# Batch 1 of a linear attention: v loaded ahead of a weight block, its kv three slots earlier, its h in whole blocks

## The chip, the cores and the metric

The kernel runs on one core of a Trainium2 chip. The core has five engines that run side by side: TensorE (PE: matrix products), VectorE (DVE), ScalarE (ACT: activation functions and copies), GpSimd (POOL) and SyncE (SP), which issues the loads here. The metric is the time of one execution on the device, in microseconds.

## What is computed

Eight batches, eight heads, 576 rows of 64. First a linear attention, then two dense layers with a gelu between them:

```python
def phi(x):
    return np.where(x > 0, x, np.exp(x) - 1.0) + 1.0
q_p, k_p = (phi(q), phi(k))
kv = np.einsum('bhsd,bhse->bhde', k_p, v)
z = np.sum(k_p, axis=2)
num = np.einsum('bhsd,bhde->bhse', q_p, kv)
den = np.einsum('bhsd,bhd->bhs', q_p, z)[..., None] + 1e-06
x = num / den            # then heads side by side: 4608 rows of 512
h = x @ w_in             # 512 x 2048
out = gelu_tanh(h) @ w_out   # 2048 x 512
```

## The kernel before

phi(x) is computed as min(exp(x), max(x + 1, 1)): an exp on ScalarE (`exp_of`, L207), an addition with a maximum on VectorE (`linear_of`, L218) and a minimum on VectorE (`least_of`, L232). v is cast to bf16 into `vp`, which has a column of ones behind every 64 values, so that kv also yields z. `kv_paired` (L257) makes the kv products of a batch, `kv_evac` (L287) copies them to the block-diagonal `kvbd`.

A batch's first 512 rows are four chunks of 128. For each chunk `nab` (L317, called `n` in the plan) multiplies the transposed q by `kvbd` into the pair of banks `ps_a`, and VectorE divides by the last column: a reciprocal and a product, which give x (L307, L309). `ps_a` exists once. `transpose_x` (L338, called `t`) transposes x on TensorE into a bank and ScalarE copies it to `xt`. The remaining 64 rows of each batch are gathered in `xt_rest`.

Then comes the dense part, `iteration(j)` (L661), for batch j: 16 blocks "h" (four matmuls of 128x512 each, and a gelu on ScalarE) and 16 steps "o" (four matmuls each: a tile t of 128 rows against a quarter u of w_out). In iteration 0 the o steps run quarter by quarter, u outside and t inside, so w_out's block u is first needed at slot 16 + 4u; in iteration 1 eight h come first, then eight o. There are 32 such slots in an iteration. The steps of the next batch's attention are hung behind slots by `at(j, slot, fn)` (L441) and run there in the order of their registration (`run`, L445). Each engine executes its instructions in the order in which this program emits them; the order of the engines among each other follows from semaphores.

Batch 0 is worked off by `first_batch` (L377) at the start, with some products on zeros to keep TensorE busy (`keep_warm`). There h's first three blocks are begun chunk by chunk as `h_quarter` (L363), four matmuls of width 128 for each chunk of xt. Batch 1 is planned by `plan_second` (L449) into iteration 0: `maps` behind slot 15 (exps, additions, minima, and a part of the casts of w_out), `transpose_q` behind slot 23, the casts of v behind 25, kv behind 26, n and t from slot 27 on, with quarters of two h blocks between them in slots 30 and 31.

All loads are issued by SP in the order of the code (L147 to L172), into the pool `pld` of seven buffers, which are handed round: a load waits until the eighth tile before it has been read. Weights come as fp32 in eight blocks of 1024 KB and are cast to bf16 by `cast_w_in` and `cast_w_out` (L136, L142), most of them on GpSimd. w_out's third block is index 2 in the code (quarter u = 2), its fourth is index 3.

Of the kernel before, what the change touches and what calls it, by code (L numbers as in the profile page):

```python
# [9 lines left out]
BF16 = mybir.dt.bfloat16  # L10
# [5 lines left out]
def kernel(  # L16
# [21 lines left out]
    C = 4  # L38
# [50 lines left out]
    def load_pairs(name, src, b, us=slice(0, NP)):  # L89
        s = src[b].rearrange("h s d -> (h s d)").rearrange("(u n f) -> n u f", n=P, f=J * D)  # L90
        nc.sync.dma_start(out=ld[name, b][:, us, :], in_=s[:, us, :])  # L91

    def load_q_paired(b, parities=(0, 1)):
        src = q[b, :, 0:MAIN, :].rearrange("(u a) (p c) d -> p a u (c d)", a=2, c=C)
        for a in parities:
            nc.sync.dma_start(out=ld["q", b][:, NP * a : NP * (a + 1), :], in_=src[:, a])  # L96
# [33 lines left out]
    def load_w(wr, i):  # L130
        t = pld.tile([P, 4, 512], FP32, name="w_st", tag="ld")
        w_st[wr is w_in_r, i] = t
        src = wr[:, :, 512 * i : 512 * (i + 1)] if wr is w_in_r else wr[:, 4 * i : 4 * i + 4, :]
        nc.sync.dma_start(out=t, in_=src)
# [15 lines left out]
    for n in "qkv":  # L150
        ld_tile(n, 0)
    for s in range(2):
        load_pairs("k", k, 0, halves[s])
        load_q_paired(0, (s,))
    for s in range(2):
        load_pairs("v", v, 0, halves[s])
    for i in range(4):
# [4 lines left out]
    load_w(w_out_r, 1)  # L162
    ld_tile("k", 1)
    load_pairs("k", k, 1)
    load_w(w_out_r, 2)
    ld_tile("v", 1)
    load_pairs("v", v, 1)
    load_w(w_out_r, 3)
    load_batch(2)
    load_main("q", q, 3)  # L170
    load_main("k", k, 3)
# [186 lines left out]
    def gelu(g, m, h_ps):  # L358
        nc.scalar.activation(g[:, m, :], h_ps, AF.Gelu_apprx_tanh)  # L359

    h_begun = {0: {}, 1: {}}

    def h_quarter(j, c, blocks):  # L363
        for m in range(blocks):
            if c == 0:
                h_begun[j][m] = bank("h_ps", [P, MAIN])
            h_mm(h_begun[j][m], xts[j], m, slice(P * c, P * (c + 1)))

    def xt_chunk(j, c):
        return xts[j][:, :, P * c : P * (c + 1)]  # L370
# [6 lines left out]
    def first_batch():  # L377
        w_ps = bank("w_ps", [P, 512])

        def keep_warm(n):  # L380
            for _ in range(n):
                nc.tensor.matmul(w_ps, lhsT=warm[:, 0:P], rhs=warm)  # L382

        qt = pt.tile([P, C, NP, P], BF16, name="qt")
        qs = (slice(0, 4), slice(4, 8))

        def transpose_q(s, fn):
            t_ps = bank("t_ps", [P, C, 2, P], BF16)
            for i in range(2):
                for c in range(C):  # L390
                    h = 4 * s + 2 * i
                    nc.tensor.transpose(
                        t_ps[:, c, i, :], phi["q", 0][:, c, h : h + 2, :], ident
                    )
            fn(out=qt[:, :, 2 * s : 2 * s + 2, :], in_=t_ps)

        keep_warm(18)
        for s in range(2):
            for n, hs in (("k", halves[s]), ("q", qs[s])):
                exp_of(n, 0, hs)  # L400
                linear_of(n, 0, hs)
                least_of(n, 0, hs)
        transpose_q(0, nc.scalar.copy)
        keep_warm(10)
        transpose_q(1, nc.scalar.copy)
        keep_warm(2)
        for ii in range(2):
            cast_v_paired(0, halves[ii], nc.vector.tensor_copy)
        for ii in range(2):
            kv_ps = [bank("kv_ps", [P, E]) for _ in range(2)]  # L410
            kv_paired(0, ii, lambda a, ii: kv_ps[a])
            for a, fn in enumerate((nc.vector.tensor_copy, nc.scalar.copy)):
                block = slice(2 * a + ii, 2 * a + ii + 1)
                kv_evac(0, block, kv_ps[a].rearrange("p (i e) -> p i e", i=1), fn)
        gelu_table()
        for s in range(2):
            cast_w_in(0, nc.gpsimd.tensor_copy, slice(256 * s, 256 * s + 256))
        for i in range(1, 4):
            cast_w_in(i, nc.gpsimd.tensor_copy)
        for i in range(2):  # L420
            cast_w_out(i, nc.gpsimd.tensor_copy)
        cast_w_out(2, nc.gpsimd.tensor_copy, slice(0, 2))
        keep_warm(2)

        xts[0] = pt.tile([P, NP, MAIN], BF16, name="xt")
        x = {0: nab(qt[:, 0], 0), 1: nab_in_banks(qt[:, 1], 0)}
        for c in range(C):
            transpose_x(x[c], xt_chunk(0, c), nc.scalar.copy)
            if c + 2 < C:
                x[c + 2] = (nab, nab_in_banks)[c % 2](qt[:, c + 2], 0)  # L430
            if c > 0:
                h_quarter(0, c - 1, 3)
        h_quarter(0, C - 1, 3)

    first_batch()

# [12 lines left out]
    def plan_second():  # L449
        b = 1  # L450
        x = {}

        def maps():
            for n in "qk":
                exp_of(n, b)
            gelu_table()
            for n in "qk":
                linear_of(n, b)
            least_of("q", b)
            cast_w_out(2, nc.vector.tensor_copy, slice(2, 4))  # L460
            least_of("k", b)

        def transpose_q():
            qts[b] = pt.tile([P, C, NP, P], BF16, name="qt")
            for s in range(2):
                t_ps = bank("t_ps", [P, 2, NP, P], BF16)
                for c in range(2):
                    for i in range(NP):
                        nc.tensor.transpose(  # L469
                            t_ps[:, c, i, :],  # L470
                            phi["q", b][:, 2 * s + c, 2 * i : 2 * i + 2, :],
                            ident,
                        )
                nc.scalar.copy(qts[b][:, 2 * s : 2 * s + 2], t_ps)

        def casts():
            cast_v_paired(b, halves[0], nc.vector.tensor_copy)
            cast_v_paired(b, halves[1], nc.scalar.copy)

        def kv():  # L480
            kv_ps = [bank("kv_ps", [P, 2, E]) for _ in range(2)]
            for ii in range(2):
                kv_paired(b, ii, lambda a, ii: kv_ps[a][:, ii, :])
            for a, fn in enumerate((nc.vector.tensor_copy, nc.scalar.copy)):
                kv_evac(b, slice(2 * a, 2 * a + 2), kv_ps[a], fn)

        def last_w_out():
            cast_w_out(3, nc.scalar.copy, slice(0, 1))
            cast_w_out(3, nc.vector.tensor_copy, slice(1, 2))
            cast_w_out(3, nc.gpsimd.tensor_copy, slice(2, 4))  # L490

        def n(c):
            x[c] = nab(qts[b][:, c], b)

        def t(c):
            if c == 0:
                xts[b] = pt.tile([P, NP, MAIN], BF16, name="xt")
            transpose_x(x[c], xt_chunk(b, c), nc.scalar.copy)

        at(0, 15, maps)  # L500
        at(0, 23, transpose_q)
        at(0, 25, casts)
        at(0, 26, kv)
        at(0, 26, last_w_out)
        at(0, 27, n, 0)
        at(0, 28, n, 1)
        at(0, 28, t, 0)
        at(0, 29, n, 2)
        at(0, 29, t, 1)
        at(0, 30, h_quarter, b, 0, 2)  # L510
        at(0, 30, n, 3)
        at(0, 30, t, 2)
        at(0, 31, h_quarter, b, 1, 2)
        at(0, 31, t, 3)
        at(0, 31, h_quarter, b, 2, 2)
        at(0, 31, h_quarter, b, 3, 2)

    def plan_prepare(b, s_linear, s_exp):
        rest = b % 2 == 0
# [141 lines left out]
    def iteration(j):  # L661
        xt = xts[j] if j < B else xt_rest
        g = pg.tile([P, MM, MAIN], BF16, name="g")
        hs = [("h", m) for m in range(MM)]
        if j == 0:
            steps = hs + [("o", t, u) for u in range(4) for t in range(C)]
        elif j == 1:
            os = [[("o", t, u) for u in us for t in range(C)] for us in ((0, 1), (2, 3))]
            steps = hs[:8] + os[0] + hs[8:] + os[1]
        else:  # L670
            steps = hs + [("o", t, u) for t in range(C) for u in range(4)]
        o_pss = {}
        for slot, step in enumerate(steps):
            if step[0] == "h":
                m = step[1]
                h_ps = h_begun.get(j, {}).get(m)
                if h_ps is None:
                    h_ps = bank("h_ps", [P, MAIN])
                    h_mm(h_ps, xt, m)
                gelu(g, m, h_ps)  # L680
            else:
                t, u = step[1:]
                if j == B and t == C - 1:
                    if u == 0:
                        last_tile(g, t)
                    continue
                if u == 0:
                    o_pss[t] = bank("o_ps", [P, d_model])
                o_mm(o_pss[t], g, t, u)
                if u == 3:  # L690
                    finish(j, t, o_pss[t])
            run(j, slot)
# [55 lines left out]
```

## Time and profile before

| what | us |
|---|---|
| median of 3 runs (289.17 to 289.42) | 289.2 |
| the profiled execution | 288.86 |
| its span | 286.9 |
| TensorE busy | 278.5 |
| ScalarE busy | 164.7 |
| VectorE busy | 107.8 |
| GpSimd busy | 18.4 |

The profile is of one execution. Busy times are sums over the span; a time such as "at 42.1" is counted from the span's start. In TensorE's timeline the durations of neighbouring matmuls overlap, since they are pipelined; the distance of two starts tells what the first one occupied. Loads keep the DMA engines full for the first 46 us (some 400 GB/s), and less after that. Iteration 0 runs from about 19 to 50 us, iteration 1 to about 80.

### The profile page before, as it was taken

How to read it: one execution, taken by the hardware profiler on the slowest of the kernel's cores; microseconds unless marked ns; L12 is line 12 of the kernel's file. 1: busy time of each engine (PE TensorE's matmuls, PEld its weight loads, DVE VectorE, ACT ScalarE, POOL GpSimd, SP SyncE). 2: the span in 40 equal slices, each digit the busy share in tenths (PEclk: the TensorE clock that was granted, in tenths of full speed). 3: DMA queues.
4: the chain of work that ended last, by engine and by line, in shares of the span. 5: the costliest groups of instructions: out<-in, count | busy, mean ns of one | idle time of the engine just before them, and what ended most of it. 6: DMA issues, size and time to landing. Idle time of an engine off the chain costs nothing.

```text
span 286.9 us, 4569 instructions
## 1 busy us (share of the span) xinstructions
PE 278.5 (97%) x1868; PEld 137.0 (48%) x1868; DVE 107.8 (38%) x180; ACT 164.7 (57%) x226; POOL 18.4 (6%) x25
## 2 busy tenths in 40 slices
PE   8789999999999999999999999999999999999994
PEld 2464456545445445544554455444544444444443
DVE  3850366633865282544247515640412010000001
ACT  4767886695966844684367735772572275027400
POOL 6066230000000000000000000000000000000000
PEclk9999999999999999999999999999999999999999
DMA  7999999956988969955799489735141210120022
GB/s 252 403 407 397 410 400 269 347 215 172 178 234 295 239 159 141 379 153 146 211 294 210 74 250 356 95 91 165 35 41 39 88 58 0 54 91 3 0 73 73
DMA packets 71379, 53.76 MB, mean 187 GB/s; under 512 B 42048, under 2 KB 62784, under 8 KB 71360
## 3 DMA queue, kind: packets, MB, share of 16 engines
q1 hardware_dynamic: 68656, 44.58, 55.4%
q10 hardware_dynamic: 2704, 8.91, 8.5%
q8 instruction: 14, 0.23, 0.3%
q14 instruction: 5, 0.04, 0.0%
HBM read 36.70 MB, written 9.44 MB: 161 GB/s over the span
## 4 chain that ended last, share of the span: by engine, by line
PE 93%; DMA 3%; DVE 1%; SPq 1%; ACT 1%; issue 0%; ACTq 0%
PE h_ps L349 44%; PE o_ps L642 43%; DMA v_x<-in_v_dram 3%; PE n_ps L294 3%; PE kv_ps L278 1%; PE t_ps L341 1%; SPq L91 1%; PE kv_ps L263 0%; SPq L96 0%; PE t_ps L469 0%; DVE x L330 0%; DVE vp L241 0%; DVE x L309 0%; ACT w_out_sb L143 0%; ACT xt L342 0%
## 5 line engine op out<-in xcount | busy, mean ns | idle before, releaser
L642 PE MATMUL o_ps<-w_out_sb,g 128*128 128x512 bf16 (+1 forms) x592 | 127.1, 373 | 0.2 <-ACT w_out_sb L143 0.2
L349 PE MATMUL h_ps<-xt,w_in_sb 128*128 128x512 bf16 (+1 forms) x572 | 118.0, 357 | 0.2 <-ACT xt L342 0.2
L359 ACT ACTIVATE g<-h_ps 128x512 bf16<-128x512 f32 x144 | 84.9, 597 | 46.6 <-PE h_ps L349 45.5
L642 PEld LDWEIGHTS <-g 128*128 128x128 bf16 x592 | 57.6, 98 | 65.4 <-issue 0.3
L349 PEld LDWEIGHTS <-w_in_sb 128*128 128x128 bf16 x636 | 57.5, 98 | 59.5 <-issue 0.7
L608 ACT COPY o_sb<-o_ps 128x512 f32<-128x512 f32 (+1 forms) x19 | 10.9, 574 | 61.5 <-PE o_ps L642 54.4
L608 DVE COPY o_sb<-o_ps 128x512 f32<-128x512 f32 (+1 forms) x18 | 12.1, 674 | 69.0 <-PE o_ps L642 69.0
L307 DVE RECIPROCAL r<-n_ps 128x8 f32<-128x8 f32 x34 | 7.0, 207 | 48.7 <-PE n_ps L294 48.7
L309 DVE TENSOR_TENSOR x<-n_ps,r 128x512 bf16<-128x512 f32 x34 | 23.5, 692 | 1.2
L212 ACT ACTIVATE k_e<-k_x 128x2048 bf16<-128x2048 f32 (+2 forms) x9 | 15.8, 1755 | 3.7 <-DMA k_x<-in_k_dram 3.7
L236 DVE TENSOR_TENSOR q_p<-q_p,q_e 128x2048 bf16<-128x2048 bf16 (+1 forms) x9 | 10.0, 1106 | 16.8 <-ACT q_e L212 16.5
L212 ACT ACTIVATE q_e<-q_x 128x2048 bf16<-128x2048 f32 (+1 forms) x9 | 15.5, 1721 | 0.5 <-DMA q_x<-in_q_dram 0.4
L349 PE MATMUL h_ps<-xt_rest,w_in_sb 128*128 128x512 bf16 x64 | 14.0, 379 | 0.0
L223 DVE TENSOR_SCALAR q_p<-q_x 128x2048 bf16<-128x2048 f32 (+1 forms) x9 | 9.9, 1100 | 10.0 <-DMA q_x<-in_q_dram 10.0
L223 DVE TENSOR_SCALAR k_p<-k_x 128x2048 bf16<-128x2048 f32 (+2 forms) x9 | 10.2, 1137 | 8.9 <-DMA k_x<-in_k_dram 8.9
L294 PEld LDWEIGHTS <-qt 128*128 128x128 bf16 x128 | 9.7, 98 | 7.0 <-DVE x L309 0.8
L294 PE MATMUL n_ps<-kvbd,qt 128*128 128x130 bf16 x128 | 12.7, 221 | 0.0
L290 DVE CAST kvbd<-kv_ps 64x260 bf16<-64x260 f32 (+2 forms) x18 | 6.6, 366 | 11.2 <-PE kv_ps L278 8.2
L236 DVE TENSOR_TENSOR k_p<-k_p,k_e 128x2048 bf16<-128x2048 bf16 (+2 forms) x9 | 10.2, 1132 | 1.4 <-ACT k_e L212 1.4
L382 PE MATMUL w_ps<-warm 128*128 128x512 bf16 x32 | 9.4, 449 | 1.2 <-DVE warm L177 1.2
L373 ACT ACT_TABLE_LOAD x8 | 10.3, 1283 | 0.1
L212 ACT ACT_TABLE_LOAD x8 | 10.3, 1283 | 0.1
(49 smaller groups left out, 95.3 us busy)
## 6 DMA issues: line engine op xcount, KB each, us to landing
out_dram<-o_sb ACTq DMA_DIRECT2D x16, 512.0 KB, 3.3
q_x<-in_q_dram SPq DMA_DIRECT2D x6, 1024.0 KB, 6.8
k_x<-in_k_dram SPq DMA_DIRECT2D x6, 1024.0 KB, 11.1
v_x<-in_v_dram SPq DMA_DIRECT2D x6, 1024.0 KB, 7.3
w_st<-in_moe_w_in_dram SPq DMA_DIRECT2D x4, 1024.0 KB, 14.0
w_st<-in_moe_w_out_dram SPq DMA_DIRECT2D x4, 1024.0 KB, 13.2
q_x<-in_q_dram SPq DMA_DIRECT2D x4, 512.0 KB, 9.3
k_x<-in_k_dram SPq DMA_DIRECT2D x2, 576.0 KB, 5.0
```

Source lines behind the costliest of these rows:

```text
L212: nc.scalar.activation(by_chunk(exps[name, b], hs), x[:, hs].rearrange("p h (c d) -> p h c d", d=D), AF.Exp,)
L223: nc.vector.tensor_scalar(by_chunk(phi[name, b], hs), x[:, hs].rearrange("p h (c d) -> p h c d", d=D), 1.0, 1.0, op0=ALU.add, op1=ALU.max,)
L236: nc.vector.tensor_tensor(p, p, e, op=ALU.min)
L294: nc.tensor.matmul(ns[i // 2][rows, 2 * E * (i % 2) : 2 * E * (i % 2 + 1)], lhsT=qt_c[:, i, rows], rhs=kvbd[:, i, :], skip_group_check=True,)
L307: nc.vector.reciprocal(r, n_v[:, :, :, D])
L309: nc.vector.tensor_tensor(x_view(x, paired), n_v[:, :, :, 0:D], r[:, :, :, None].to_broadcast([P, 2, NP, D]), op=ALU.mult,)
L349: nc.tensor.matmul(h_ps[:, ts], lhsT=w_in_sb[:, c, P * m : P * (m + 1)], rhs=xt[:, c, ts], start=(c == 0), stop=(c == KM - 1), skip_group_ ...
L359: nc.scalar.activation(g[:, m, :], h_ps, AF.Gelu_apprx_tanh)
L373: nc.scalar.preload_act_table_set("gelu_apprx_tanh_and_others")
L382: nc.tensor.matmul(w_ps, lhsT=warm[:, 0:P], rhs=warm)
L608: (nc.scalar.copy if on_scalar else nc.vector.tensor_copy)(dst, src)
L642: nc.tensor.matmul(o_ps, lhsT=g[:, m, P * t : P * (t + 1)], rhs=w_out_sb[:, m, fs], start=(m == 0), stop=(m == MM - 1),)
```

## The change

It has these parts.

- At the start, the loads of batch 0 go q half, k half, q half, k half, where before k's half came first in each pair; the exps, additions and minima of batch 0 follow in the same order.
- Batch 1's v is loaded ahead of w_out's third block.
- The third block's first half is cast on GpSimd within `maps`, behind the cast of the second half of batch 1's v, which moves from ScalarE to GpSimd. The first half of that v is cast on VectorE between the minima of q and k. VectorE casts the third block's second half behind k's minimum.
- The transposes of batch 1's q go to the pair of banks `ps_a` in one tile; kv stands right behind them, at slot 23. The gelu table is loaded behind kv's evacuation.
- n goes to slots 24 to 27, t to slots 25 to 28; within a slot, t of one chunk stands ahead of n of the next.
- w_out's fourth block is cast in halves on GpSimd and ScalarE, without VectorE.
- Batch 1 has no quarters of h: its blocks are all computed with width 512. Batch 0 keeps its own.

```diff
--- before.py
+++ after.py
@@ -150,8 +150,8 @@
     for n in "qkv":
         ld_tile(n, 0)
     for s in range(2):
+        load_q_paired(0, (s,))
         load_pairs("k", k, 0, halves[s])
-        load_q_paired(0, (s,))
     for s in range(2):
         load_pairs("v", v, 0, halves[s])
     for i in range(4):
@@ -162,10 +162,10 @@
     load_w(w_out_r, 1)
     ld_tile("k", 1)
     load_pairs("k", k, 1)
-    load_w(w_out_r, 2)
     ld_tile("v", 1)
     load_pairs("v", v, 1)
-    load_w(w_out_r, 3)
+    for i in range(2, 4):
+        load_w(w_out_r, i)
     load_batch(2)
     load_main("q", q, 3)
     load_main("k", k, 3)
@@ -358,13 +358,13 @@
     def gelu(g, m, h_ps):
         nc.scalar.activation(g[:, m, :], h_ps, AF.Gelu_apprx_tanh)
 
-    h_begun = {0: {}, 1: {}}
-
-    def h_quarter(j, c, blocks):
+    h_begun = {}
+
+    def h_quarter(c, blocks):
         for m in range(blocks):
             if c == 0:
-                h_begun[j][m] = bank("h_ps", [P, MAIN])
-            h_mm(h_begun[j][m], xts[j], m, slice(P * c, P * (c + 1)))
+                h_begun[m] = bank("h_ps", [P, MAIN])
+            h_mm(h_begun[m], xts[0], m, slice(P * c, P * (c + 1)))
 
     def xt_chunk(j, c):
         return xts[j][:, :, P * c : P * (c + 1)]
@@ -396,7 +396,7 @@
 
         keep_warm(18)
         for s in range(2):
-            for n, hs in (("k", halves[s]), ("q", qs[s])):
+            for n, hs in (("q", qs[s]), ("k", halves[s])):
                 exp_of(n, 0, hs)
                 linear_of(n, 0, hs)
                 least_of(n, 0, hs)
@@ -419,7 +419,6 @@
             cast_w_in(i, nc.gpsimd.tensor_copy)
         for i in range(2):
             cast_w_out(i, nc.gpsimd.tensor_copy)
-        cast_w_out(2, nc.gpsimd.tensor_copy, slice(0, 2))
         keep_warm(2)
 
         xts[0] = pt.tile([P, NP, MAIN], BF16, name="xt")
@@ -429,8 +428,8 @@
             if c + 2 < C:
                 x[c + 2] = (nab, nab_in_banks)[c % 2](qt[:, c + 2], 0)
             if c > 0:
-                h_quarter(0, c - 1, 3)
-        h_quarter(0, C - 1, 3)
+                h_quarter(c - 1, 3)
+        h_quarter(C - 1, 3)
 
     first_batch()
 
@@ -453,29 +452,24 @@
         def maps():
             for n in "qk":
                 exp_of(n, b)
-            gelu_table()
-            for n in "qk":
                 linear_of(n, b)
             least_of("q", b)
+            cast_v_paired(b, halves[0], nc.vector.tensor_copy)
+            cast_v_paired(b, halves[1], nc.gpsimd.tensor_copy)
+            least_of("k", b)
+            cast_w_out(2, nc.gpsimd.tensor_copy, slice(0, 2))
             cast_w_out(2, nc.vector.tensor_copy, slice(2, 4))
-            least_of("k", b)
 
         def transpose_q():
             qts[b] = pt.tile([P, C, NP, P], BF16, name="qt")
-            for s in range(2):
-                t_ps = bank("t_ps", [P, 2, NP, P], BF16)
-                for c in range(2):
-                    for i in range(NP):
-                        nc.tensor.transpose(
-                            t_ps[:, c, i, :],
-                            phi["q", b][:, 2 * s + c, 2 * i : 2 * i + 2, :],
-                            ident,
-                        )
-                nc.scalar.copy(qts[b][:, 2 * s : 2 * s + 2], t_ps)
-
-        def casts():
-            cast_v_paired(b, halves[0], nc.vector.tensor_copy)
-            cast_v_paired(b, halves[1], nc.scalar.copy)
+            t_ps = ps_a.tile([P, C, NP, P], BF16, name="t_ps", tag="a")
+            for c in range(C):
+                for i in range(NP):
+                    nc.tensor.transpose(
+                        t_ps[:, c, i, :], phi["q", b][:, c, 2 * i : 2 * i + 2, :], ident
+                    )
+                if c % 2 == 1:
+                    nc.scalar.copy(qts[b][:, c - 1 : c + 1], t_ps[:, c - 1 : c + 1])
 
         def kv():
             kv_ps = [bank("kv_ps", [P, 2, E]) for _ in range(2)]
@@ -483,11 +477,11 @@
                 kv_paired(b, ii, lambda a, ii: kv_ps[a][:, ii, :])
             for a, fn in enumerate((nc.vector.tensor_copy, nc.scalar.copy)):
                 kv_evac(b, slice(2 * a, 2 * a + 2), kv_ps[a], fn)
+            gelu_table()
 
         def last_w_out():
-            cast_w_out(3, nc.scalar.copy, slice(0, 1))
-            cast_w_out(3, nc.vector.tensor_copy, slice(1, 2))
-            cast_w_out(3, nc.gpsimd.tensor_copy, slice(2, 4))
+            cast_w_out(3, nc.gpsimd.tensor_copy, slice(0, 2))
+            cast_w_out(3, nc.scalar.copy, slice(2, 4))
 
         def n(c):
             x[c] = nab(qts[b][:, c], b)
@@ -499,21 +493,11 @@
 
         at(0, 15, maps)
         at(0, 23, transpose_q)
-        at(0, 25, casts)
-        at(0, 26, kv)
+        at(0, 23, kv)
+        for c in range(C):
+            at(0, 24 + c, n, c)
+            at(0, 25 + c, t, c)
         at(0, 26, last_w_out)
-        at(0, 27, n, 0)
-        at(0, 28, n, 1)
-        at(0, 28, t, 0)
-        at(0, 29, n, 2)
-        at(0, 29, t, 1)
-        at(0, 30, h_quarter, b, 0, 2)
-        at(0, 30, n, 3)
-        at(0, 30, t, 2)
-        at(0, 31, h_quarter, b, 1, 2)
-        at(0, 31, t, 3)
-        at(0, 31, h_quarter, b, 2, 2)
-        at(0, 31, h_quarter, b, 3, 2)
 
     def plan_prepare(b, s_linear, s_exp):
         rest = b % 2 == 0
@@ -673,7 +657,7 @@
         for slot, step in enumerate(steps):
             if step[0] == "h":
                 m = step[1]
-                h_ps = h_begun.get(j, {}).get(m)
+                h_ps = h_begun.get(m) if j == 0 else None
                 if h_ps is None:
                     h_ps = bank("h_ps", [P, MAIN])
                     h_mm(h_ps, xt, m)
```

## The prediction

> **What bounds the kernel now.** I read the chain of work that ended last first, then TensorE's timeline, then the timelines of VectorE, GpSimd and the loads.
>
> The shares of the chain, from the page:
>
> ```profile
> PE 93%; DMA 3%; DVE 1%; SPq 1%; ACT 1%; issue 0%; ACTq 0%
> ```
>
> So TensorE is the path from the first kv product to the end. DMA's 3% is the start: the first kv waits for the second half of batch 0's v. An edit can move the time in three ways only: through the start, through what TensorE has to do, or through gaps between its instructions. I looked for gaps at the places of the diff, by the start times on TensorE's timeline (start, duration, instruction, count, idle before it). Durations there overlap, so I take differences of starts.
>
> ```profile
> 38.55 1.06 PE L469 MATMUL t_ps<-ident,q_p 128*128 128x128 bf16 x16
> 39.45 2.75 PE L642 MATMUL o_ps<-w_out_sb,g 128*128 128x512 bf16 x12
> 42.13 0.78 PE L263 MATMUL kv_ps<-vp,k_p 64*64 64x65 bf16 x72
> 42.84 1.04 PE L642 MATMUL o_ps<-w_out_sb,g 128*128 128x512 bf16 x4
> 43.71 0.40 PE L294 MATMUL n_ps<-kvbd,qt 128*128 128x130 bf16 x4
> 44.29 1.02 PE L642 MATMUL o_ps<-w_out_sb,g 128*128 128x512 bf16 x4 [0.18 <-ACT w_out_sb L143]
> 45.15 0.40 PE L294 MATMUL n_ps<-kvbd,qt 128*128 128x130 bf16 x4
> 45.39 0.38 PE L341 MATMUL t_ps<-ident,x 128*128 128x128 bf16 x4
> 45.61 1.03 PE L642 MATMUL o_ps<-w_out_sb,g 128*128 128x512 bf16 x4
> 46.58 0.41 PE L294 MATMUL n_ps<-kvbd,qt 128*128 128x130 bf16 x4
> ...
> 51.18 5.79 PE L349 MATMUL h_ps<-xt,w_in_sb 128*128 128x128 bf16 x32 [0.23 <-ACT xt L342]
> 56.80 7.07 PE L642 MATMUL o_ps<-w_out_sb,g 128*128 128x512 bf16 x32
> ```
>
> A block of o (four matmuls) takes 0.86 from start to start, four transposes 0.22, an n 0.24, kv 0.71 (42.13 to 42.84). The stage from 38.55 to 56.80 lasts 18.25. Its work without any gap, with h as whole blocks, is 0.89 (16 transposes) + 0.71 (kv) + 8 x 0.864 = 6.91 (32 matmuls of o) + 4 x 0.235 = 0.94 (n) + 0.88 (t) + 6.91 (eight blocks of h) = 17.24. So 1.01 us is lost here now. I find it again as 0.09 before kv, 0.36 before the o at 44.29 (a ScalarE cast of w_out's fourth block), 0.11 before the n at 46.58, 0.39 before 51.18 (the last chunk of xt), and 0.06 for quarters of h. The last: eight 128-wide matmuls take 0.445 (47.91 to the n at 48.35), 32 of them 1.78; eight 512-wide ones 1.73.
>
> VectorE there:
>
> ```profile
> 35.70 1.23 DVE L236 TENSOR_TENSOR q_p<-q_p,q_e 128x2048 bf16<-128x2048 bf16 x1 [0.42 <-ACT q_e L212]
> 36.84 1.53 DVE L143 CAST w_out_sb<-w_st 128x1024 bf16<-128x1024 f32 x1
> 38.29 1.34 DVE L236 TENSOR_TENSOR k_p<-k_p,k_e 128x2304 bf16<-128x2304 bf16 x1
> 39.56 0.75 DVE L241 CAST vp<-v_x 128x1152 bf16<-128x1152 f32 x1
> 43.03 0.60 DVE L290 CAST kvbd<-kv_ps 64x130 bf16<-64x130 f32 x2 [2.72 <-PE kv_ps L263]
> 45.59 0.21 DVE L307 RECIPROCAL r<-n_ps 128x8 f32<-128x8 f32 x1 [0.50 <-PE n_ps L294]
> 45.83 0.69 DVE L309 TENSOR_TENSOR x<-n_ps,r 128x512 bf16<-128x512 f32 x1
> ```
>
> and GpSimd:
>
> ```profile
> 36.50 1.32 POOL L143 CAST w_out_sb<-w_st 128x1024 bf16<-128x1024 f32 x1 [3.59 <-DMA w_st<-in_moe_w_out_dram]
> 41.90 1.04 POOL L143 CAST w_out_sb<-w_st 128x1024 bf16<-128x1024 f32 x1 [4.08 <-DMA w_st<-in_moe_w_out_dram]
> ```
>
> Two things are to be seen. From n's start at 45.15 its x is done at 46.52 on VectorE (45.83 + 0.69), and the next n, which needs the same two banks, starts at 46.58: n to x to TensorE costs 1.43. And casts on VectorE and GpSimd disturb each other: GpSimd's 1024-wide cast takes 1.04 alone and 1.32 while VectorE's minimum runs; VectorE's 1024-wide cast shows 1.53 and ends 0.55 after GpSimd's, where a 1152-wide one alone takes 0.75.
>
> **What the Trainium skill says.** "SBUF — State Buffer", Who interferes with whom: VectorE's 2-port casts, and its operations with two SBUF inputs, contend with GpSimd for a pair of ports; whoever starts first keeps it for the whole instruction and the other blocks. The rows above agree (1.32 against 1.04; 1.53). "TensorE: Matmul & The Clock Gate", Step-by-step: what each phase is for: matmuls stay in program order, only weight loads are pulled ahead. The trace agrees: idle gaps stand where the code puts the waiting step. The same page, Part 1: the clock falls after an idle window of some 3.4 us; the granted clock is 1.00 in all stretches of before, with gaps up to 0.92 in the start. "DMA: Bandwidth & Descriptors", Queues, rings and completion order: one queue's descriptors are taken in ring order on each engine. The landings agree: batch 1's k 33.91, third block 36.5, v 39.3 (issued 25.93, 13.4 to landing), fourth block 41.9.
>
> **The change part by part.**
>
> *q halves ahead of k's.* The same six loads, other order; the second v half lands at 12.3 as before, and VectorE's cast of it (12.35, after 0.20 of waiting) releases the second kv. With k last, k's second exp (1.16) starts at about 9.5, its minimum is done at about 11.5, the first v cast at 12.2: still ahead of the landing. TensorE's transposes come earlier and it waits longer before kv. Cost 0; bounds: -0.15 (v cast at once at 12.2) to +0.2; the idle stretch of about 1.6 is under the clock's window.
>
> *v ahead of w_out's third block.* At 2.85 for v's 1152 KB (36.48 to 39.33), v lands at 33.91 + 2.85 = 36.76, the third block 2.57 later at 39.33, the fourth at 41.9 as now. On SP v's load waits for the second w_in cast, done at 19.4 and so long ago, and what is queued behind SP's loads keeps its bytes and order.
>
> *maps, casts, kv at slot 23.* exp, additions and q's minimum stay where they are. Then at about 36.8 GpSimd takes v's second half. Its price is not in the trace; from 1.04 for 1024 and 1.89 for 2048 it is 0.19 + 1.152 x 0.83 = 1.15 if the odd output step costs nothing (taken), up to double, 2.3. VectorE's first half is blocked behind it, as its w_out cast is now: end 37.95 + 0.62 = 38.57. k's minimum follows, 38.49 to 39.83, so kv starts at 39.87. The transposes of q end at 39.44: a wait of 0.43. Were VectorE first, k's minimum would be the one blocked, with some 0.2 more; were nothing blocked it would end at 39.04 and cost nothing. Queued behind the wait is all of TensorE.
>
> The third block, landed at 39.33, is the new tight one. GpSimd's half waits for k's minimum (39.76) and ends at about 40.8; VectorE's half is blocked until then and ends at 41.36; kv's evacuation stands behind it on VectorE and ends at 41.89. TensorE: kv 39.87 to 40.58, o with the third block from 40.85 (0.27 lost), its second half from 41.40 (0.12), the first n at 41.93 (0.10). Sum with kv 0.92. Without blocking: kv at 39.44, casts done at 40.4, 0.30 lost.
>
> ScalarE: the gelu table moves from 37.70 behind kv's evacuation, about 41.7 to 43.0, in time where ScalarE has nothing due before xt's first copy; the copies of qt are done at 41.1 as now. The fourth block's ScalarE half is cast by about 46.3 and is used at about 47. Cost 0; if late, some tenths.
>
> *n and t.* This is the largest term. Before, a slot ran n(c+1) ahead of t(c): between an n and the next step that needs its x lay a t and an o, 0.22 + 0.86, and later a quarter of h. Now each slot is o, t(c), n(c+1): only the o lies between n(c) and t(c). n 0.24 + o 0.86 = 1.10 against 1.43: 0.33 lost at each of four t, 1.32. VectorE has little else then, so nothing shortens it.
>
> *Quarters gone.* Their 0.06 and the last wait (0.39) go: t(3) now comes three blocks of o, 2.59, ahead of h, which hides its ScalarE copy of 0.59. The other waits of before (0.09, 0.36, 0.11) go too, as the order is new.
>
> Sum: -1.01 + 0.92 + 1.32 = +1.23. Checked forward: n at 41.93, t(0) at 43.36, then 1.65 for each of three more t, 48.31; + 0.22 + 2.59 + 6.91 = 58.03 against 56.80. Behind it VectorE's and ScalarE's work for batch 2 moves along and loads get more slack; TensorE shows no gap that could take it back, so it reaches the end whole. On the profiled execution (288.86, span 286.9) this gives 290.1; that one lies 0.34 under the median 289.2, on which I put the same +1.23: 290.4.
>
> **The rivals.**
> - A, as summed: 290.4, own range 290.1 to 290.8. Chance 0.55.
> - B, casts do not block each other: 0.30 instead of 0.92, so +0.6, 289.8. For it: GpSimd's spans are rough. Against: both long casts above. 0.20, half of it within 0.2% (0.58 us, about what a measurement of this kernel tells from no change).
> - C, GpSimd's v cast is slow, 2.3: everything from kv on 1.15 later, +2.4, 291.6. For it: the output's odd step, which no GpSimd row shows. Against: VectorE and ScalarE run it at their usual rate (0.75, 1.18). 0.15.
> - D, the four t do not wait: the chain n to t is hidden, at slots 25 to 28. It decides below: with B's 0.30, the change gains once the wait at each t is under 0.18, n to t under 1.28; at none, -0.71 and 288.5. For it: the idle shown there now is small, and before's sum of gaps does go. Against: 1.43 is read from this same chain. 0.10, of it 0.03 within 0.2%.
>
> **How the numbers follow.** Slower: A 0.55, C 0.15, half of B 0.10 = 0.80. Same: 0.10 + 0.03 = 0.13. Faster: 0.07. The range leaves out D and the end of C: 289.5 (B with the start's 0.15 and a little less blocking) to 291.6.
>
> **What would show it.** In the new trace: v landed near 36.8 and the third block near 39.3; four transposes t each idle about 0.3 on VectorE's x; kv starting at 39.9 rather than 39.45; an o waiting for a w_out cast near 40.8; the h blocks of batch 1 without gaps; the o after them at about 58.0; kv of batch 0 still at 13.16. Wrong if the t show no idle time, if kv waits past 40.5, or if the first o moves from 31.65.

## The result and the profile after

| | median us | ratio to before, 95% |
|---|---|---|
| before (6 runs) | 289.05 | |
| changed (6 runs) | 289.91 | 1.0028, 1.0015 to 1.0040 |

The changed kernel is slower by 0.86 us. Its profiled execution took 289.97 (span 288.2), against 288.86 (286.9) before. The interval of the ratio means +0.4 to +1.2 us.

TensorE's timeline of the changed kernel, the same stage as before (start, duration, instruction, count, idle before it):

```profile
37.91 0.61 PE L468 MATMUL t_ps<-ident,q_p 128*128 128x128 bf16 x8
39.62 0.61 PE L468 MATMUL t_ps<-ident,q_p 128*128 128x128 bf16 x8 [1.10 <-ACT qt L472]
40.15 0.78 PE L263 MATMUL kv_ps<-vp,k_p 64*64 64x65 bf16 x72
40.87 0.38 PE L626 MATMUL o_ps<-w_out_sb,g 128*128 128x512 bf16 x1
41.42 0.59 PE L626 MATMUL o_ps<-w_out_sb,g 128*128 128x512 bf16 x2 [0.17 <-DVE w_out_sb L143]
41.93 0.41 PE L294 MATMUL n_ps<-kvbd,qt 128*128 128x130 bf16 x4
42.17 1.02 PE L626 MATMUL o_ps<-w_out_sb,g 128*128 128x512 bf16 x4
43.37 0.40 PE L341 MATMUL t_ps<-ident,x 128*128 128x128 bf16 x4 [0.17 <-DVE x L309]
...
45.02 0.40 PE L341 MATMUL t_ps<-ident,x 128*128 128x128 bf16 x4 [0.17 <-DVE x L309]
...
51.17 7.07 PE L349 MATMUL h_ps<-xt,w_in_sb 128*128 128x512 bf16 x32
58.07 4.26 PE L626 MATMUL o_ps<-w_out_sb,g 128*128 128x512 bf16 x18
```

(The first o shows three of its four matmuls; one record is missing.) The stage now lasts from 37.91 to 58.07, 20.16 us, where it was 18.25. Against the 17.24 of its work, 2.92 are lost: 1.35 around the transposes of q (2.24 from 37.91 to 40.15, for 0.89 of work), 0.20 in the first o, and 1.33 ahead of the four t; 0.04 are spread. A t should follow its o after 0.86, at 43.03; it starts at 43.37. Of these 0.34 only 0.17 are printed as idle, since the last matmul's modelled end overlaps the wait; that is why starts are compared.

The stage is longer by 1.91, but it begins 0.64 earlier. The gain is from the start: the second of batch 0's two kv groups on TensorE, in the kernel before

```profile
13.16 0.48 PE L263 MATMUL kv_ps<-vp,k_p 64*64 64x65 bf16 x36 [0.17 <-DVE vp L241]
```

and both groups in the changed one:

```profile
11.65 0.48 PE L263 MATMUL kv_ps<-vp,k_p 64*64 64x65 bf16 x36 [1.15 <-DVE vp L241]
12.51 0.48 PE L263 MATMUL kv_ps<-vp,k_p 64*64 64x65 bf16 x36 [0.39 <-DVE vp L241]
```

The halves of v landed at 10.9 and 12.3 before and at 10.3 and 11.7 after (issue plus time to landing), and VectorE's cast of the second half started at once both times (12.35 and 11.70). 1.91 - 0.64 is 1.27, and from 58.07 to the end it is 230.1 in both: nothing behind the stage gives or takes.

VectorE and GpSimd of the changed kernel, in this order:

```profile
36.93 0.77 DVE L241 CAST vp<-v_x 128x1152 bf16<-128x1152 f32 x1 [0.35 <-DMA v_x<-in_v_dram]
37.61 2.31 DVE L236 TENSOR_TENSOR k_p<-k_p,k_e 128x2304 bf16<-128x2304 bf16 x1
39.84 1.52 DVE L143 CAST w_out_sb<-w_st 128x1024 bf16<-128x1024 f32 x1
```
```profile
36.96 1.75 POOL L241 CAST vp<-v_x 128x1152 bf16<-128x1152 f32 x1 [3.87 <-DMA v_x<-in_v_dram]
39.50 1.31 POOL L143 CAST w_out_sb<-w_st 128x1024 bf16<-128x1024 f32 x1 [0.79 <-DMA w_st<-in_moe_w_out_dram]
```

k's minimum takes 2.31 where it took 1.34. VectorE's cast of v started first. The record of GpSimd's lasts until 38.71, 1.01 behind the end of VectorE's (37.70), and the minimum ends 1.21 behind that (39.92): the times fit three instructions that ran one after the other. The chain of waits, by engine, gives less to TensorE than the 93% of before:

```profile
PE 82%; DMA 10%; DVE 3%; SPq 2%; issue 1%; POOL 0%; ACT 0%
```

Ahead of the o at 41.42 it runs through VectorE's cast of the third block and k's minimum back to the load of batch 1's v (issued 23.90, landed 36.91).

### The profile page after: what moved, and what is told of

Read it like the earlier page. It is cut to its first block, busy times and chain, and to the rows that moved or that the text cites. A ratio compares the mean times of both kernels' runs of the same rounds, so it can differ in the third digit from the quotient of the medians.

```text
span 288.2 us, 4493 instructions
## 1 busy us (share of the span) xinstructions
PE 276.8 (96%) x1816; PEld 135.9 (47%) x1844; DVE 108.0 (37%) x179; ACT 164.2 (57%) x225; POOL 19.7 (7%) x26
## 4 chain that ended last, share of the span: by engine, by line
PE 82%; DMA 10%; DVE 3%; SPq 2%; issue 1%; POOL 0%; ACT 0%
PE o_ps L626 39%; PE h_ps L349 38%; DMA w_st<-in_moe_w_in_dram 6%; DMA v_x<-in_v_dram 5%; PE n_ps L294 3%; PE kv_ps L278 1%; SPq L134 1%; DVE x L309 1%; DVE k_p L236 1%; SPq L91 1%; PE t_ps L341 1%; DVE w_out_sb L143 1%; SPq L96 0%; DVE r L307 0%; POOL w_in_sb L137 0%
## 5 line engine op out<-in xcount | busy, mean ns | idle before, releaser
L349 PE MATMUL h_ps<-xt,w_in_sb 128*128 128x512 bf16 (+1 forms) x533 | 116.2, 364 | 0.8 <-issue 0.2
L349 PEld LDWEIGHTS <-w_in_sb 128*128 128x128 bf16 x612 | 56.3, 98 | 59.9 <-issue 0.4
L592 ACT COPY o_sb<-o_ps 128x512 f32<-128x512 f32 (+1 forms) x19 | 10.9, 575 | 60.9 <-PE o_ps L626 53.8
L236 DVE TENSOR_TENSOR k_p<-k_p,k_e 128x2048 bf16<-128x2048 bf16 (+2 forms) x9 | 11.2, 1240 | 0.8 <-ACT k_e L212 0.7
L212 ACT ACT_TABLE_LOAD x8 | 10.3, 1283 | 0.1
L373 ACT ACT_TABLE_LOAD x8 | 10.3, 1283 | 0.1
## 6 DMA issues: line engine op xcount, KB each, us to landing
k_x<-in_k_dram SPq DMA_DIRECT2D x6, 1024.0 KB, 10.6
```

Of the source, the lines that this page charges most:

```text
L212: nc.scalar.activation(by_chunk(exps[name, b], hs), x[:, hs].rearrange("p h (c d) -> p h c d", d=D), AF.Exp,)
L236: nc.vector.tensor_tensor(p, p, e, op=ALU.min)
L349: nc.tensor.matmul(h_ps[:, ts], lhsT=w_in_sb[:, c, P * m : P * (m + 1)], rhs=xt[:, c, ts], start=(c == 0), stop=(c == KM - 1), skip_group_ ...
L373: nc.scalar.preload_act_table_set("gelu_apprx_tanh_and_others")
L592: (nc.scalar.copy if on_scalar else nc.vector.tensor_copy)(dst, src)
```

## The experiments

All ratios are to the kernel before, measured alongside.

| run | median us | ratio, 95% |
|---|---|---|
| q first alone | 288.14 | 0.9968, 0.9958 to 0.9977 |
| k first, rest changed | 290.48 | 1.0056, 1.0038 to 1.0073 |
| n ahead of t | 289.19 | 1.0012, 1.0004 to 1.0020 |
| v half on ScalarE | 289.99 | 1.0037, 1.0024 to 1.0049 |
| transposes first | 289.94 | 1.0036, 1.0024 to 1.0049 |
| transposes first, v half on ScalarE | 289.87 | 1.0030, 1.0019 to 1.0042 |
| the same, halves swapped, n ahead | 288.92 | 0.9998, 0.9990 to 1.0006 |
| q first, whole blocks | 288.63 | 0.9989, 0.9981 to 0.9998 |
| q first, two waits mended | 287.66 | 0.9960, 0.9947 to 0.9973 |
| q first in the loads only | 290.07 | 1.0049, 1.0033 to 1.0065 |

### The change in two parts

The first part done alone on the kernel before:

```diff
     for s in range(2):
+        load_q_paired(0, (s,))
         load_pairs("k", k, 0, halves[s])
-        load_q_paired(0, (s,))
...
-            for n, hs in (("k", halves[s]), ("q", qs[s])):
+            for n, hs in (("q", qs[s]), ("k", halves[s])):
```

> The kernel before with the change's first part alone: batch 0's q halves loaded and worked off ahead of k's. Theory: the second half of batch 0's v lands near 11.75 instead of 12.24, so the second kv starts near 12.51 instead of 13.16 and the stage of the o steps, which in this plan is paced by TensorE, passes most of it on: 288.4 to 288.6, ratio to before 0.998. Rival 1, the earlier start is eaten by waits for loads (v at 39.3, w_out's fourth block at 41.9): 289.0, same as before. Rival 2, the earlier landing is chance of one execution and not of the order: second kv at 13.16 again, 289.0.

It gained 0.32%, about 0.9 us, a little more than expected. Its trace is of the slowest of its 19 executions (288.60) and shows less: v's second half landed at 11.9, the second kv began at 12.78, and the o after h at 56.54 instead of 56.80. The landing varies from one execution to the next: in the traces of ten kernels with q loaded first (the changed one and nine of these runs) v's second half landed between 11.6 and 12.3, nine of them by 12.0, and in the two with k first at 12.3 and 12.5. So it is the medians (288.14 of 19 runs against 288.95 of 34) that show the gain to be no chance.

The opposite, the changed kernel with this part undone (the same lines, other way round):

> The changed kernel with the first part undone: k halves ahead of q's again. Theory: from kv of batch 1 on the stage is paced by loads (k 34, v 36.8, third block 39.4), not by when TensorE arrives; TensorE arrives 0.65 later, waits 0.65 less, the first n stays at 41.9, and the time stays at 289.9 (at most 0.15 more). Rival, the parts add up: 0.65 slower than the changed kernel, 290.5.

My theory fell; the rival had it. The rest of the change alone costs 0.56%, 1.6 us, and the two parts add up: 1.0056 x 0.9968 = 1.0024, within the interval of the changed kernel. TensorE's timeline of this run says why most of the earlier start is not eaten:

```profile
38.69 0.61 PE L468 MATMUL t_ps<-ident,q_p 128*128 128x128 bf16 x8
40.40 0.61 PE L468 MATMUL t_ps<-ident,q_p 128*128 128x128 bf16 x8 [1.10 <-ACT qt L472]
40.94 0.78 PE L263 MATMUL kv_ps<-vp,k_p 64*64 64x65 bf16 x72
41.65 1.04 PE L626 MATMUL o_ps<-w_out_sb,g 128*128 128x512 bf16 x4
42.52 0.40 PE L294 MATMUL n_ps<-kvbd,qt 128*128 128x130 bf16 x4
```

kv follows the first transposes after 2.25 here and after 2.24 in the changed kernel. What TensorE waits for is not a load but its own product: the second eight transposes go into the same tile as the first eight, and wait until ScalarE has copied those out (1.10 of idle time in both). This wait moves with TensorE. The o shows no gap any more, as the third block's casts are done by then (VectorE's at 41.40). So TensorE, which begins the transposes 0.78 later here, is 0.59 later at the first n.

### The four waits of t

```diff
         for c in range(C):
             at(0, 24 + c, n, c)
+        for c in range(C):
             at(0, 25 + c, t, c)
```

> The changed kernel with n of the next chunk ahead of t of this one within each slot (the same slots). Theory: each t has n's 0.24 more between it and its x, and the distance of two n falls from 1.66 to n-to-x-to-n's 1.43; the four gaps of 0.33 become one of 0.33 and three of about 0.11, the stage ends 0.6 to 0.7 earlier, 289.2 to 289.3. Rival, what costs is the late third block of w_out and the gaps behind it are cover for it: under 0.2 gained, 289.7 or more.

289.19, against 289.91 for the changed kernel: 0.7 by the medians, 0.5 by the ratios (1.0012 against 1.0028). In the traces the stage lasts 19.55 (37.83 to 57.38) instead of 20.16, 0.61 less, as the theory said. TensorE's timeline of this run:

```profile
43.34 0.41 PE L294 MATMUL n_ps<-kvbd,qt 128*128 128x130 bf16 x4 [0.17 <-DVE x L309]
...
44.78 0.41 PE L294 MATMUL n_ps<-kvbd,qt 128*128 128x130 bf16 x4
```

From n to n 1.44 (43.34 to 44.78), against 1.66 from t to t in the changed kernel (43.37 to 45.02). The work is the same; the t now stands behind the n, in time that was idle.

### What holds the first n

Three waits stand ahead of it: the transposes' for the copy, kv's for k's minimum, and o's for the casts of the third block. First GpSimd's cast of v goes to ScalarE:

```diff
-            cast_v_paired(b, halves[1], nc.gpsimd.tensor_copy)
+            cast_v_paired(b, halves[1], nc.scalar.copy)
```

> The changed kernel with the second half of batch 1's v cast on ScalarE (as before the change) instead of GpSimd; ScalarE is idle from 37.0 to 38.5. Theory of the shared ports: the minimum of k, 2.31 now, takes 1.34 and ends near 38.95; but the second group of q's transposes still waits for ScalarE's copy of the first (39.62), so kv starts at 40.15 as now and only VectorE's cast of the third block and kv's evacuation come earlier; the first n near 41.6 to 41.9, total 289.6 to 289.9. Rival, k's minimum is what holds kv: kv at 39.5, n at 41.2, total 289.2.

k's minimum fell from 2.31 to 1.35, as in this line of VectorE's timeline:

```profile
37.50 1.35 DVE L236 TENSOR_TENSOR k_p<-k_p,k_e 128x2304 bf16<-128x2304 bf16 x1
```

and kv stayed at 40.25, the first n at 41.87, the total at 289.99. The blocking between VectorE and GpSimd is real and costs nothing here. Then the copies go behind all transposes:

```diff
-                if c % 2 == 1:
-                    nc.scalar.copy(qts[b][:, c - 1 : c + 1], t_ps[:, c - 1 : c + 1])
+            for c in (1, 3):
+                nc.scalar.copy(qts[b][:, c - 1 : c + 1], t_ps[:, c - 1 : c + 1])
```

> The changed kernel with all 16 transposes of batch 1's q ahead of both of ScalarE's copies. Theory 1: the second group no longer waits (1.10 of idle time goes), but kv then waits for k's minimum (ends at 39.92), and o for the casts of the third block (41.36): kv near 39.96 instead of 40.15, the first n still at 41.9, total 289.8 to 289.9. Rival: the wait of the transposes is the loss, 1.1 gained, 288.8.

The 1.10 are gone from the transposes, but kv waits 0.80 for k's minimum and starts at 39.92; the first n is at 41.97. With this order ScalarE's first copy starts 1.10 after the first transpose (39.16 to 38.06), once all sixteen are through; before, where each group of eight had a tile of its own, it started after 0.65 (39.20 to 38.55). So it looks as if the order between the engines is kept for the whole tile and not for each of its banks. The changed kernel with two tiles was not run. Both edits together:

> The changed kernel with the transposes of q ahead of the copies and the second half of v cast on ScalarE, so that neither the copy nor k's minimum holds kv. Theory 1: kv near 38.9, 1.2 earlier, but the third block lands at 39.4 and its first half is cast on GpSimd until about 41.0 behind VectorE's half; o waits there and the first n stays near 41.9: 289.8 to 290.0, nothing gained. Rival: the three waits add up, and with two of them gone the kernel is 1.0 to 1.2 faster, 288.8.

Nothing gained, though kv is 1.2 earlier. TensorE, then GpSimd:

```profile
38.99 0.78 PE L263 MATMUL kv_ps<-vp,k_p 64*64 64x65 bf16 x72
41.08 1.02 PE L626 MATMUL o_ps<-w_out_sb,g 128*128 128x512 bf16 x4 [1.31 <-POOL w_out_sb L143]
```
```profile
39.46 1.57 POOL L143 CAST w_out_sb<-w_st 128x1024 bf16<-128x1024 f32 x1 [6.41 <-DMA w_st<-in_moe_w_out_dram]
```

The first n is at 41.9 to 42.0 in all four (41.93, 41.87, 41.97, 41.94). In the changed kernel k's minimum would release kv only 0.2 before TensorE's own wait does, and the third block, which is loaded behind v, lands at 39.4 to 39.5 and is cast by 41.0 to 41.4. The three end at nearly the same time, so that taking away one or two shows the next. So the third block, which landed at 36.5 before, seems to be the price of loading v first; no run changed the order of these two loads alone. Last, the cast's halves were exchanged so that VectorE's, which is done first, is the one needed first, with n ahead of t as above:

```diff
-            cast_w_out(2, nc.gpsimd.tensor_copy, slice(0, 2))
-            cast_w_out(2, nc.vector.tensor_copy, slice(2, 4))
+            cast_w_out(2, nc.vector.tensor_copy, slice(0, 2))
+            cast_w_out(2, nc.gpsimd.tensor_copy, slice(2, 4))
```

> The kernel of the preceding run with two more edits: VectorE casts the third block's first half and GpSimd its second, and n goes ahead of t within a slot. Theory 1: o's first matmuls start near 40.1 and its last pair near 41.0, the first n near 41.45, 0.4 earlier; n ahead of t gains 0.7 as in the run that did it alone; total 288.7 to 288.9. Rival, the cast of the third block is not what o waits for: only the 0.7, 289.2.

288.92, equal to before and within what the theory said. The o started at 40.18, but the first n at 41.56, and half of it waited until 41.99 for ScalarE's part of kv's evacuation, which now stands behind the copies of q: a fourth wait at the same place. In this trace the start came late too (v's second half at 12.3, the second kv at 13.09).

### The start, and better kernels

Is it the order of the loads or that of the work? The loads alone:

```diff
     for s in range(2):
+        load_q_paired(0, (s,))
         load_pairs("k", k, 0, halves[s])
-        load_q_paired(0, (s,))
```

> The kernel before with only the loads of batch 0 in the order q, k, q, k; exps, additions and minima stay in the order k, q. Theory: v still lands 0.3 to 0.6 earlier than before, since that follows from the order of the loads, but VectorE and ScalarE take k's second half, which lands last, ahead of q's, so VectorE reaches the casts of v later and the second kv starts at 13.1 or later: 288.9 to 289.3, nothing gained. Rival, the order of the loads is enough: second kv near 12.6, 288.3.

1.0049: it costs 1.4 us, more than expected. v landed somewhat earlier all the same (10.6 and 12.0), but VectorE and ScalarE begin with k, which now comes second (at 6.38, where the changed kernel begins with q at 4.62), and VectorE reaches v's casts late:

```profile
12.58 1.43 DVE L241 CAST vp<-v_x 128x1152 bf16<-128x1152 f32 x2
```

In the changed kernel these casts start at 10.84. So the order of the loads is not enough: the loads bring v earlier, and the work in the order of the landings lets VectorE be there. The order of the work alone was not run.

Where v's lead arises can be read from the landings of the six loads: 4.6, 6.0, 7.4, 8.8, 10.3 and 11.7 in the changed kernel, but 4.4, 5.7, 8.1, 9.5, 10.9 and 12.3 before. With k first there are 2.4 us between the second and the third, with q first 1.35 (2.3 in the other trace with k first, 1.35 to 1.4 in the other nine with q first). Why was not found. It is hardly bandwidth (252 and 403 GB/s in the page's first two slices before, 250 and 410 after). And what v gains is gone soon after: GpSimd's cast of w_in's second block, which waits for its load, starts at 18.23 instead of 17.56, and that of the third at 20.70 in both. No matmul shows a wait for it: the first o still starts 0.65 earlier (31.00 against 31.65).

From this a better kernel follows, the old plan with the first part. One attempt took batch 1's quarters away and moved kv forward:

```diff
-        at(0, 26, kv)
-        at(0, 27, n, 0)
+        at(0, 24, casts)
+        at(0, 24, kv)
+        at(0, 25, n, 0)
...
-        at(0, 30, h_quarter, b, 0, 2)
...
-        at(0, 31, h_quarter, b, 3, 2)
```

(The gelu table also goes behind slot 30, VectorE casts all of v, and GpSimd and ScalarE the fourth block.)

> The kernel before with q's halves first (the run of that part alone), the old order of loads, and batch 1 without quarters: v cast on VectorE alone, kv behind slot 24, n in slots 25 to 28 each ahead of t, t in 26 to 29, the gelu table behind slot 30. Theory: kv near 40.95 (casts of v end there; v lands at 39.4), gaps of about 0.1 at three n, three blocks of h less cut up, no wait for the last chunk of xt since two blocks of o lie behind the last t; the stage loses 0.5 to 0.6 instead of 1.1: 287.6 to 287.8. Rival, the fourth block (42.0) or the casts hold o: 288.1 or more.

288.63: hardly better than before, worse than the first part alone, as the rival said. I had taken TensorE's arrival from the kernel before; with the early start it was ready for kv at about 39.8, and v's casts ended at 41.0. kv began at 40.36, when the first half was there, and took 1.1 instead of 0.71. The other attempt kept the plan and mended two of its waits:

```diff
-            cast_w_out(3, nc.scalar.copy, slice(0, 1))
-            cast_w_out(3, nc.vector.tensor_copy, slice(1, 2))
-            cast_w_out(3, nc.gpsimd.tensor_copy, slice(2, 4))
+            cast_w_out(3, nc.gpsimd.tensor_copy, slice(0, 2))
+            cast_w_out(3, nc.vector.tensor_copy, slice(2, 3))
+            cast_w_out(3, nc.scalar.copy, slice(3, 4))
...
-        at(0, 31, h_quarter, b, 1, 2)
         at(0, 31, t, 3)
+        at(0, 31, h_quarter, b, 1, 2)
```

> The kernel before with q's halves first (the run of that part alone), and two waits of its stage mended: the fourth block of w_out is cast with its first half on GpSimd, its third quarter on VectorE and its last on ScalarE, and the last t stands ahead of the second quarters of h instead of behind them. Theory: the o after the first n no longer waits for ScalarE's cast (0.37), and the last chunk of xt is copied beside two groups of quarters (0.40 of waiting becomes 0.1 at t): 0.5 to 0.6 under the run with q first alone, 287.6. Rival, VectorE's quarter of the cast delays x of the first chunk by 0.4 and takes half of it back: 287.9.

287.66, ratio 0.9960 to before: faster than both kernels of the study. Over the first part alone the gain is small: 0.2 by the ratios, whose intervals overlap, 0.5 by the medians, and in the traces the stage lasts 18.08 (38.09 to 56.17) instead of 18.36, 0.28 less. On its TensorE

```profile
43.35 0.40 PE L294 MATMUL n_ps<-kvbd,qt 128*128 128x130 bf16 x4
43.58 1.02 PE L642 MATMUL o_ps<-w_out_sb,g 128*128 128x512 bf16 x4
44.78 0.41 PE L294 MATMUL n_ps<-kvbd,qt 128*128 128x130 bf16 x4 [0.17 <-DVE x L309]
...
49.65 6.68 PE L349 MATMUL h_ps<-xt,w_in_sb 128*128 128x128 bf16 x47
56.17 4.05 PE L642 MATMUL o_ps<-w_out_sb,g 128*128 128x512 bf16 x18
```

the o follows the first n at once, and h runs from 49.65 on in 6.5 without a gap. But the second n now waits 0.34 (43.58 + 0.86 to 44.78), and not for the rival's reason. VectorE:

```profile
43.79 0.21 DVE L307 RECIPROCAL r<-n_ps 128x8 f32<-128x8 f32 x1
```

The reciprocal starts 0.44 after its n, as before the change (43.71 to 44.15) and at the next n (44.78 to 45.22), so VectorE's quarter of the cast delayed nothing. From n to n it is 1.43 here, 1.44 before and 1.47 with q first alone: the way from n through x to the next n takes that long in each of them, and the wait for ScalarE's cast had only stood in front of this one. Mending it was worth at most 0.04; nearly all of what was gained is the last t's.

## Why the prediction was right, and where it was not

The direction held, the size in part: +1.23 was forecast, and 0.86 is measured between the medians and 1.27 between the stages of the two traces (whose executions took 288.86 and 289.97, 1.11 apart). The measured 289.91 lies in the whole range, 289.5 to 291.6, but below the 290.1 to 290.8 of rival A, whose mechanism it is; B's 289.8 is nearer by number alone. The traced execution of before was quicker than that kernel's medians (289.05 and 289.2), that of the changed kernel was not (289.91). Why executions of one kernel differ is not shown.

The loads landed as worked out (v at 36.9, the third block at 39.5, forecast 36.8 and 39.3), and so did the path from there: VectorE's cast of the third block ends at 41.36 as forecast, the first n stands at 41.93 as forecast, and the o after h at 58.07 (forecast 58.03). But two terms of the sum were mis-sized, and that they cancel is luck. In the changed kernel TensorE's own way, with the early start and the wait that I had overlooked, would have allowed the n at 41.73 (40.87 + 0.86), just ahead of the cast. With the start as I had it (the run with k first), this way is the longer one: the n stands at 42.52, and the change costs 1.6. Two of my own signs had turned: the first o moved from 31.65 to 31.00, and batch 0's second kv from 13.16 to 12.51.

- *q halves ahead of k's*, put at 0 with a bound of -0.15: it gains 0.64 in the trace, and 0.9 done alone. I took v's landing as fixed at 12.3 because the six loads have the same bytes in any order. It moved by 0.65, to 11.7. My bound of 12.2 for VectorE's cast fell with it: it rested on k's second exp at 9.5, which began at 8.87, since the fourth load landed earlier too (8.8 instead of 9.5).
- *kv's wait*, 0.43 for k's minimum: 1.35 are lost from the first transposes to kv, and the releaser is ScalarE's copy of q. I counted the 16 transposes as 0.89 in one piece, though a copy stands between the two groups; the second group waits until it is done. In the changed kernel k's minimum would have let kv go 0.2 earlier, no more.
- *The third block*: 0.27 + 0.12 forecast, 0.20 found, as TensorE came later to it than I thought (kv at 40.15, not 39.87). With the other waits gone it is the bound (1.31 idle).
- *The four t*: 1.32 forecast, 1.33 found. The run with n ahead confirms it: about 0.6 of it can be had by order alone.
- *Waits and quarters of before*, 1.01: gone as forecast; h runs in 6.90 for eight blocks.
- *Casts blocking each other*: as "SBUF — State Buffer", Who interferes with whom, in the Trainium skill states, one operation blocks the other for its whole length; this fits the trace (k's minimum 2.31 beside GpSimd's cast, 1.35 without it). VectorE came first, not GpSimd, which I had as the variant. It was real, but taking it away at v's cast gained nothing (289.99), since other waits end within 0.2 of it; so rival B's 0.6 does not follow from it. GpSimd's odd output step cost nothing either, if its cast ran from 37.70 to 38.71 (1.01), as far as GpSimd's spans can be trusted, which speaks against rival C. Rival D falls with the t.
- *Clock*: the idle stretch before kv was 1.15, and the granted clock is 0.999 over the span.

## What to carry to other kernels

Where a step needs another engine's answer, count what stands between the two in program order: here a transpose behind one o waited 0.33 each time, and exchanging the two steps gave back about 0.6 us. Where several waits end within some tenths of each other, removing one shows the next, as it did at the first n and in the last run at the second; find the latest by removing two or three together before deciding what a change costs. Split a change into its parts: here one half gained 0.9 us and the other lost 1.6, and the better kernel was one of the halves.

## What was unexpected

With the same bytes in the queue, the order of the loads in front of v moved its landing by 0.65 us between the two main traces; over all twelve it is 11.6 to 12.3 with q first and 12.3 and 12.5 with k first. And two groups of transposes into the two banks of one tile did not overlap with the copy between them: 1.10 us idle in all four traces where a copy stood between the groups.
